# Layer 1's first ten weight quadrants decoded beside layer 0's output products, kept in DRAM, with layer 1's input sums issued twice as fast

## The chip, the cores and the metric

The kernel runs on one NeuronCore of a Trainium2 chip. The metric is the device time in microseconds (us) of one execution. The engines are named as in the profile: PE is TensorE (matmuls; PEld its weight loads), DVE is VectorE, ACT is ScalarE, POOL is GpSimd, and SP is SyncE, which here issues nearly all transfers between DRAM and SBUF, in order, in one queue.

## What is computed

```python
x = attention(q, k, v)            # 4 batches, 12 heads, 448 tokens, head 64, with rms norms and a softmax
x = x.transpose(0, 2, 1, 3).reshape(1792, 768)
x = (x @ w_a) * (x @ w_b) @ w_out                        # layer 0: 768 -> 1536 -> 768
out = (sigmoid(x @ w_gate) * (x @ w_val)) @ w_out2       # layer 1, same sizes
```

The six weight matrices lie in DRAM as 64-bit floats. Everything else is 32-bit.

## The kernel before

**The products.** Each layer has a first part (x times its two left matrices) and a second part (the gated product times the output matrix). Every matrix product is done on quadrants by a scheme of Strassen's kind: seven products of sums of quadrants (passes 1, 2, 5, 3, 6, 7, 4) in place of eight. A 32-bit operand is split into a rounded part and a rest (names ending in h and l, or hi and lo), and each product is three matmuls: high by high, low by high, high by low. So DVE and ACT have to make, for each operand of PE, a cast (ACT: `wh`, `xh`, `gh`) and a subtraction (DVE: `wl`, `xl`, `gl`, in `rest`, line 615).

**First part** (`first_part`, matmuls in line 938). It is a list of 84 events (m, p), m being one of 12 column blocks (even: first matrix, odd: second) and p the pass. An event is 18 matmuls: six steps (two column halves of 512 and 384, by three chunks) of three. The events begin

```python
[(0, 1), (1, 1), (0, 2)] + [(2, 1), (1, 2), (3, 1), (2, 2), (3, 2)] + [(0, 5), (0, 6), (1, 5), (0, 7), (0, 3), ...]
```

and are called e0, e1, ... below: e0 is (0, 1), e4 is (1, 2), e6 is (2, 2), e7 is (3, 2), e8 is (0, 5), e9 is (0, 6), e11 is (0, 7). Passes 1 and 2 share a PSUM bank: after pass 1 of a column block ACT copies the bank away (`u<-mm`, line 990), and pass 2 of the same block adds into the bank, so it cannot begin before that copy. Likewise pass 7 waits for the copy of pass 6 (line 994). e7 thus waits for the copy of e5's bank, e11 for that of e9's. Passes 1 and 2 use quadrants of x as they are; passes 5, 6, 7 and 3 need the sums S1, S2, S3 and S4 of quadrants, which `operands` makes for each layer: per sum three tiles of 128 x 896, each one DVE operation (line 851), one ACT cast (line 842) and one DVE rest. `operands` is advanced once at every fourth step of the first part's events (`ticks % 4`).

**Weights** (`weights`). A quadrant is loaded as pairs of 32-bit words into a `raw` tile (384 KB; two buffers, for layer 1's first ten loads also two of the eight `u` tiles) and decoded to 32-bit floats in a `d` tile by one ACT operation (line 678) and three DVE operations (lines 679, 681, 685). Then `splits` makes `wh` and `wl` of it or of a difference of two quadrants (lines 771 and 775); `wh` and `wl` have four buffers each, so the pair for an event can be written once PE is done with the event four before. `prepare` advances both, at every such step, up to two events ahead of PE. Four quadrants are stored to DRAM (`bd`) after their decoding and loaded again later. Layer 1's decodings begin in the last six groups of layer 0's second part.

**Second part** (`second_part`, line 1221 for layer 0). 42 groups, numbered k: seven passes by six chunks, in layer 0 18 matmuls each. `beside` loads the gated products (`u<-gd`) and the decoded output weights (`d<-wd`), combines them for the pass (lines 1095, 1116) and splits them. At the end of a pass ACT copies the three banks away, and finished quadrants of the result are split into layer 1's operands (`xh`, `xl`). `tick` is called after each three matmuls.

All engines run in order, each through its own list; a row that waits holds everything behind it on that engine.

Of the kernel before, what the change touches and what calls it, by code (L numbers as in the profile page):

```python
# [23 lines left out]
def attention_then_two_gated_mlps(  # L24
# [84 lines left out]
    xd = in_dram("xd", S2, 1, 2, KD)  # L109
    gd = in_dram("gd", S2, 2, 5, HF)  # L110
    wd = in_dram("wd", HB, 2, 6, HF)
    bd = in_dram("bd", HB, 2, 2, 2)


    def attention():
# [516 lines left out]
    Q11, Q12, Q21, Q22 = QUADS = (0, 0), (0, 1), (1, 0), (1, 1)  # L632
    NEEDS = {1: Q11, 5: Q12, 2: Q21, 6: Q22}
    W, done, preps = {}, [-1, -1], [None, None]

    def weights(l):

        plan = []
        events = orders[l]
        k = 0  # L640
        for e, (m, p) in enumerate(events):
            plan.append(("g", m, p))
            while k < 4 * HF and e >= 24 + 2.3 * k:
                plan.append(("o", k % HF, (Q11, Q21, Q12, Q22)[k // HF]))
                k += 1
        assert k == 4 * HF
        wanted = [
            (2, m, p) if x == "o" else (m % 2, m // 2, NEEDS[p]) for x, m, p in plan if x == "o" or p in NEEDS
        ]
        loaded = []  # L650
        total = len(wanted)

        def fill():

            while wanted and len(loaded) < (4 if total - len(wanted) < 10 and len(free_u) >= 3 else 2):
                load()

        def load():
            n, j, q = wanted.pop(0)
            tag = None  # L660
            if [t for t, _ in loaded].count(None) >= 2:
                tag, u = take_u()
                r = u[:, 0:2 * HB].bitcast(U32).rearrange("p (f w) -> p f w", w=2)
            else:
                r = rawp.tile([P, HB, 2], U32, tag="raw", name="raw")
            if n < 2:
                nc.sync.dma_start(out=r.rearrange("p (k f) w -> p k (f w)", f=P), in_=quadrant(l, n, j, q))
            else:
                nc.sync.dma_start(out=r.rearrange("p f w -> p (f w)"), in_=quadrant(l, n, j, q))
            loaded.append((tag, r))  # L670

        def decode(t):
            tag, r = loaded.pop(0)
            t = t.bitcast(U32)
            low, high = r[:, :, 0], r[:, :, 1]


            nc.scalar.activation(out=f32(t), in_=f32(high), func=AF.Copy, scale=2.0 ** -112)  # L678
            nc.vector.tensor_scalar(out=low, in0=low, scalar1=29, scalar2=None, op0=ALU.logical_shift_right)
            yield  # L680
            nc.vector.scalar_tensor_tensor(  # L681
                out=low, in0=high, scalar=0x80000000, in1=low, op0=ALU.bitwise_and, op1=ALU.bitwise_or
            )
            yield
            nc.vector.scalar_tensor_tensor(  # L685
                out=t, in0=t, scalar=3, in1=low, op0=ALU.logical_shift_left, op1=ALU.bitwise_or
            )
            if tag:
                free_u.append(tag)
            fill()  # L690
            yield

        def dec(tag):
            return decp.tile([P, HB], F32, tag=tag, name=tag)

        def less(out, a, b):
            nc.gpsimd.tensor_tensor(out=out, in0=a, in1=b, op=ALU.subtract)

        B, stores = {}, []

        def decodes():
            e = k = -1
            if l == 0:
                fill()
                yield
            else:
                for n in range(12):
                    if n % 3 == 0:
                        load()
                    yield  # L710
            for x, m, p in plan:
                now = stores[:]
                if x == "o":
                    k += 1
                    t = dec("d5" if k % 2 else "d8")
                    yield from decode(t)
                    stores.append((wd[l][QUADS.index(p)][m], t))
                else:
                    e += 1
                    if p in NEEDS:  # L720
                        q = QUADS.index(NEEDS[p])
                        spilled = 2 <= m < EARLY and p < 3
                        tag = f"d{4 * (m % 2) + (q + 1 if spilled else q)}"
                        if q == 1 and m >= EARLY:
                            tag = "d1"
                        if l == 1:
                            while held[0] is not None and tag not in held[0]:
                                yield
                            if held[0] is not None:
                                held[0].remove(tag)  # L730
                        t = dec(tag)
                        B[m, q] = t
                        yield from decode(t)
                        if spilled:
                            stores.append((bd[l][m % 2][q // 2], t))
                for dst, t in now:
                    nc.sync.dma_start(out=dst, in_=t)
                    stores.pop(0)
                decoded[l] = e
                yield  # L740
            for dst, t in stores:
                nc.sync.dma_start(out=dst, in_=t)
            decoded[l] = NE

        again = []

        def reload(m, q):
            B[m, q] = dec(f"d{4 * (m % 2) + q}")
            nc.sync.dma_start(out=B[m, q], in_=bd[l][m % 2][q // 2])

        def splits():
            last = None

            def low():
                n, *of = last
                rest(*of, nc.vector)
                done[l] = n

# [140 lines left out]
    def first_part(l, then):  # L899
# [15 lines left out]
        for e, (m, p) in enumerate(events):  # L915
# [18 lines left out]
            for o, size in HALVES:  # L934
                for c in range(KC):
                    hi, lo = X[n_][c]
                    for z, (w, x) in enumerate(((wh, hi), (wh, lo), (wl, hi))):
                        nc.tensor.matmul(  # L938
                            ps[:, o:o + size], w[:, P * c:P * c + P], x[:, o:o + size],
                            start=(p in (1, 5) and c == 0 and z == 0), stop=(c == KC - 1 and z == 2),  # L940
                            skip_group_check=p not in (1, 5),
                        )
                    prepare(l, min(e + AHEAD, NE - 1), 1)
                    if more is None and ready[0]:
                        more = operands(l)
                    if more is not None:
                        ticks += 1
                        if ticks % 4 == 0:
                            next(more, None)
                    if e >= NE - 4:  # L950
                        then(e - NE)
                    yield
# [213 lines left out]
    def second_part(l, step):  # L1166
# [19 lines left out]
            nc.vector.tensor_tensor(out=sums(x, un), in0=sums("a", un), in1=sums(x, un), op=ALU.add)  # L1186

        after, finals, beats = [], [], []

        def tick(k):  # L1190
            step(k)
            beats.append(k)
            if after and (l == 1 or len(beats) % 3 == 0):
                after.pop(0)()
            if l == 0 and k >= NS - 6:
                prepare(1, max(-1, AHEAD - NS + k), 1)

# [151 lines left out]
```

## Time and profile before

| | |
|---|---|
| median of 3 runs | 1232.35 us (1231.51, 1232.35, 1234.49) |
| profiled execution | 1234.08 us; span from first to last instruction 1232.3 us |
| mean granted clock of PE | 0.985 of full speed |
| attention and the start of layer 0 | up to about 336 us |
| layer 0, first part from there, second part | up to 604.9 us, up to 758.8 us |
| layer 1, first part, second part | up to 1071.3 us, up to 1222.6 us |

The busy time of an engine is a share of the span. PE's busy time counts matmuls from start to modelled end, which overlap: what a matmul costs is read from starts, or from how many start in a stretch.

### The profile page before, as it was taken

The numbers are of one execution on the slowest core, as the hardware profiler recorded it, in microseconds if no ns is written. First come the engines' busy times: TensorE is split into PE (matmuls) and PEld (weight loads), VectorE is DVE, ScalarE is ACT, GpSimd is POOL, SyncE is SP. The second block draws the span as 40 slices with busy tenths as digits, with TensorE's granted clock in tenths as the row PEclk, the third lists the DMA queues.
The fourth block names the chain that finished last, engine by engine and source line by source line (L and its number), as shares of the span: only waits on it lengthen the run. The fifth ranks groups of instructions, "written<-read, shape, count | busy, mean of one in ns | idle before, by whom it ended". The sixth has DMA issues, their size and how long they took to land.

```text
span 1232.3 us, 18208 instructions
## 1 busy us (share of the span) xinstructions
PE 1204.8 (98%) x6440; PEld 1018.6 (83%) x6440; DVE 917.6 (74%) x1625; ACT 655.3 (53%) x1275; POOL 157.4 (13%) x241
## 2 busy tenths in 40 slices
PE   7999999999899999999999999999999999999997
PEld 5666666667688888888888888888888888999997
DVE  6788888864976786876668689966877877666672
ACT  5787778864543434444446565544435444445552
POOL 3666667700000000000000000000000000000000
PEclk7999999999799999999999999999999999999999
DMA  4344454427134665653875754234665654677683
GB/s 132 95 130 134 127 168 130 129 66 261 48 111 130 186 196 142 197 173 126 297 255 165 222 182 141 83 99 131 190 179 165 196 156 156 237 272 239 192 260 94
DMA packets 141899, 203.01 MB, mean 165 GB/s; under 512 B 23112, under 2 KB 116464, under 8 KB 141808
## 3 DMA queue, kind: packets, MB, share of 16 engines
q1 hardware_dynamic: 141200, 201.43, 52.3%
q8 instruction: 50, 0.82, 0.3%
q10 hardware_dynamic: 480, 0.43, 0.1%
q14 instruction: 41, 0.34, 0.1%
q0 software_dynamic: 128, 0.00, 0.0%
HBM read 147.46 MB, written 54.35 MB: 164 GB/s over the span
## 4 chain that ended last, share of the span: by engine, by line
PE 67%; DVE 3%; ACT 2%; DMA 1%; issue 1%; ACTq 0%; SPq 0%; DVEq 0%
PE mm L938 45%; PE mm L1221 13%; PE mm L1231 10%; DVE xl L615 1%; DMA u<-gd 0%; DMA wd<-d 0%; DVE u L851 0%; ACT gh L1135 0%; ACT xh L842 0%; DVE al L851 0%; DVE wl L615 0%; ACTq L1287 0%; ACT mm L1202 0%; ACT ah L1258 0%; ACT u L992 0%
## 5 line engine op out<-in xcount | busy, mean ns | idle before, releaser
L938 PE MATMUL mm<-xh,wh 128*128 128x512 f32 (+1 forms) x1008 | 370.5, 368 | 4.8 <-ACT u L994 2.0
L938 PE MATMUL mm<-xl,wh 128*128 128x512 f32 (+1 forms) x1008 | 371.4, 368 | 3.5 <-DVE xl L615 3.4
L938 PE MATMUL mm<-xh,wl 128*128 128x512 f32 (+1 forms) x1008 | 372.1, 369 | 1.6 <-DVE wl L615 1.6
L938 PEld LDWEIGHTS mm<-xh,wh 128*128 128x128 f32 x1008 | 191.0, 189 | 30.6 <-ACT u L994 2.4
L938 PEld LDWEIGHTS mm<-xl,wh 128*128 128x128 f32 x1008 | 190.9, 189 | 28.3 <-DVE xl L615 5.5
L938 PEld LDWEIGHTS mm<-xh,wl 128*128 128x128 f32 x1008 | 190.9, 189 | 23.9 <-DVE wl L615 2.9
L615 DVE TENSOR_TENSOR wl<-d,wh 128x384 fp32r<-128x384 f32 x252 | 137.5, 552 | 69.3 <-ACT wh L1098 40.3
L783 ACT CAST wh<-d 128x384 fp32r<-128x384 f32 x168 | 83.0, 514 | 107.4 <-DVE d L771 75.1
L678 ACT ACTIVATE d<-raw 128x384 f32<-128x384 f32 x140 | 76.8, 554 | 80.1 <-DMA raw<-in_moe_w_out_dram 43.3
L685 DVE SCALAR_TENSOR_TENSOR d<-d,raw 128x384 uint32<-128x384 uint32 x140 | 78.7, 562 | 52.2 <-ACT d L678 46.3
L361 ACT ACTIVATE P<-s,nm 128x448 f32<-128x448 f32 x168 | 105.2, 635 | 7.4 <-DVE nm L349 7.1
L1098 ACT CAST wh<-d 128x384 fp32r<-128x384 f32 x84 | 43.2, 514 | 119.8 <-issue 36.8
L349 DVE TENSOR_REDUCE nm<-s 128x1 f32<-128x448 f32 x168 | 97.5, 614 | 4.4 <-PE s L343 4.4
L1231 PE MATMUL mm<-wh,gh 128*128 128x384 f32 x294 | 98.8, 336 | 0.3 <-ACT mm L1202 0.2
L1231 PE MATMUL mm<-wl,gh 128*128 128x384 f32 x294 | 98.6, 335 | 0.0
L1231 PE MATMUL mm<-wh,gl 128*128 128x384 f32 x294 | 98.5, 335 | 0.0
L1221 PE MATMUL mm<-gl,wh 128*128 128x512 f32 x252 | 92.6, 368 | 0.0
L1221 PE MATMUL mm<-gh,wl 128*128 128x512 f32 x252 | 92.4, 366 | 0.0
L1221 PE MATMUL mm<-gh,wh 128*128 128x512 f32 x252 | 91.7, 364 | 0.0
L390 ACT COPY pt<-tr 128x512 f32<-128x512 f32 x96 | 55.0, 573 | 49.7 <-PE tr L374 45.5
L681 DVE SCALAR_TENSOR_TENSOR raw<-raw 128x384 uint32<-128x384 uint32 x140 | 78.4, 560 | 4.0
L1008 DVE TENSOR_TENSOR u<-mm,u 128x896 f32<-128x896 f32 x48 | 52.2, 1087 | 30.7 <-PE mm L938 30.6
(155 smaller groups left out, 1947.5 us busy)
## 6 DMA issues: line engine op xcount, KB each, us to landing
gd<-u SPq DMA_DIRECT2D x60, 448.0 KB
u<-gd SPq DMA_DIRECT2D x60, 448.0 KB
d<-wd SPq DMA_DIRECT2D x132, 192.0 KB
raw<-in_moe_w_out_dram SPq DMA_DIRECT2D x48, 384.0 KB
wd<-d SPq DMA_DIRECT2D x72, 192.0 KB
raw<-in_moe_w_a_dram SPq DMA_DIRECT2D x24, 384.0 KB
raw<-in_moe_w_b_dram SPq DMA_DIRECT2D x24, 384.0 KB
raw<-in_moe_w_val_dram SPq DMA_DIRECT2D x23, 384.0 KB
```

What stands on the lines that cost most here:

```text
L349: nc.vector.tensor_reduce(out=d["nm"][:, t:t + 1], in_=d["ps"][t], axis=AX.X, op=ALU.max, negate=True)
L361: nc.scalar.activation(out=e, in_=d["ps"].pop(t), func=AF.Exp, bias=d["nm"][:, t:t + 1], accum_out=d["sum"][:, t:t + 1])
L390: nc.scalar.copy(out=d["pt"][j][:, w], in_=tr)
L615: eng.tensor_tensor(out=lo, in0=t, in1=f32(hi), op=ALU.subtract)
L678: nc.scalar.activation(out=f32(t), in_=f32(high), func=AF.Copy, scale=2.0 ** -112)
L681: nc.vector.scalar_tensor_tensor(out=low, in0=high, scalar=0x80000000, in1=low, op0=ALU.bitwise_and, op1=ALU.bitwise_or)
L685: nc.vector.scalar_tensor_tensor(out=t, in0=t, scalar=3, in1=low, op0=ALU.logical_shift_left, op1=ALU.bitwise_or)
L783: nc.scalar.copy(out=hi, in_=t)
L938: nc.tensor.matmul(ps[:, o:o + size], w[:, P * c:P * c + P], x[:, o:o + size], start=(p in (1, 5) and c == 0 and z == 0), stop=(c == KC - ...
L1008: nc.vector.tensor_tensor(out=u, in0=ps, in1=u, op=ALU.add)
L1221: nc.tensor.matmul(ps[:, o:o + size], w[:, P * un:P * un + P], g[:, o:o + size], start=(p in (1, 5) and f == 0 and z == 0), stop=(f == HF ...
L1231: nc.tensor.matmul(ps[:, o:o + HB], g[:, P * t:P * t + P], w, start=(p in (1, 5) and f == 0 and z == 0), stop=(f == HF - 1 and z == 2), sk ...
```

## The change

Ten quadrants of layer 1's left matrices, those that its first events need (in order: for e0 to e9), are decoded during layer 0's second part instead of at the seam between the layers. A generator `decode_soon` is advanced at every third `tick` of that part (18 matmuls are six ticks, so twice per group) from group 4 on. It takes one of the eight `u` tiles, loads the quadrants through the two `raw` buffers, decodes them into the tile's two halves in turn, and stores each to a DRAM tile of `pd`. At the seam layer 1 loads the decoded quadrants from `pd` (192 KB each) into their `d` tiles; the four that were spilled to `bd` are loaded again from `pd`, without a store of their own. The rule that let layer 1's first ten loads run four ahead goes. And layer 1's `operands` is advanced at every second step of the events instead of every fourth.

```diff
-    bd = in_dram("bd", HB, 2, 2, 2)
+    bd = in_dram("bd", HB, 2, 2)
+    SOON = 10
+    pd = in_dram("pd", HB, SOON)
...
+    soon = [(m % 2, m // 2, NEEDS[p]) for m, p in orders[1] if p in NEEDS][:SOON]
...
+    def decode_soon():
+        raws, late = [], []
+        n_loaded = [0]
+        def load():
+            raws.append(rawp.tile([P, HB, 2], U32, tag="raw", name="raw"))
+            load_raw(raws[-1], 1, *soon[n_loaded[0]])
+            n_loaded[0] += 1
+        def store():
+            n, t = late.pop()
+            nc.sync.dma_start(out=pd[n], in_=t)
+        load()
+        load()
+        while len(free_u) < 2:
+            yield
+        tag, spare = take_u()
+        for n in range(SOON):
+            t = spare[:, HB * (n % 2):HB * (n % 2) + HB]
+            yield from decode_steps(t, raws.pop(0))
+            late.append((n, t))
+            if n_loaded[0] < SOON:
+                load()
+            yield
+            store()
+            yield
+        free_u.append(tag)
...
+        known = {w: n for n, w in enumerate(soon)} if l else {}
         wanted = [
-            (2, m, p) if x == "o" else (m % 2, m // 2, NEEDS[p]) for x, m, p in plan if x == "o" or p in NEEDS
+            (2, m, p) if x == "o" else (m % 2, m // 2, NEEDS[p])
+            for x, m, p in plan
+            if x == "o" or p in NEEDS and (m % 2, m // 2, NEEDS[p]) not in known
         ]
...
-            while wanted and len(loaded) < (4 if total - len(wanted) < 10 and len(free_u) >= 3 else 2):
+            while wanted and len(loaded) < (4 if l == 0 and total - len(wanted) < 10 and len(free_u) >= 3 else 2):
...
-            if l == 0:
-                fill()
-                yield
-            else:
-                for n in range(12):
-                    if n % 3 == 0:
-                        load()
-                    yield
+            fill()
+            yield
...
-                        yield from decode(t)
-                        if spilled:
-                            stores.append((bd[l][m % 2][q // 2], t))
+                        if (m % 2, m // 2, NEEDS[p]) in known:
+                            nc.sync.dma_start(out=t, in_=pd[known[m % 2, m // 2, NEEDS[p]]])
+                            yield
+                        else:
+                            yield from decode(t)
+                        if spilled and l == 0:
+                            stores.append((bd[m % 2][q // 2], t))
...
-            nc.sync.dma_start(out=B[m, q], in_=bd[l][m % 2][q // 2])
+            src = pd[known[m % 2, m // 2, QUADS[q]]] if l else bd[m % 2][q // 2]
+            nc.sync.dma_start(out=B[m, q], in_=src)
...
-                        if ticks % 4 == 0:
+                        if ticks % (2 if l else 4) == 0:
...
+        soon_steps = decode_soon() if l == 0 else None
...
+            if l == 0 and 4 <= k < NS - 6 and len(beats) % 3 == 0:
+                next(soon_steps, None)
```

`load_raw` and `decode_steps` (not shown) are the old loading and decoding code as functions: in a step ACT's operation and DVE's first, in the next DVE's second, in the next DVE's third. PE's and POOL's instructions stand in the same order as before. Line numbers of the changed kernel are its own: its lines 617, 823, 882, 891, 1002, 1030 are 615, 783, 842, 851, 962, 990 of before, and its 649, 650, 652, 656 are 678, 679, 681, 685.

**DVE, start of layer 1's first part.** Before, from the weight rest of e6 (`wl<-d_8624`) over that of e7 (`wl<-d_8656`):

```order
L615 TENSOR_TENSOR wl<-d_8624,wh 128x384
L679 TENSOR_SCALAR raw<-raw 128x384
L681 SCALAR_TENSOR_TENSOR raw<-raw 128x384
L685 SCALAR_TENSOR_TENSOR d_8770<-d_8770,raw 128x384
L615 TENSOR_TENSOR xl<-al,xh 128x896
L851 TENSOR_TENSOR u_8787<-al,ah 128x896
L851 TENSOR_TENSOR al<-ah,al 128x896
L962 TENSOR_TENSOR u_8715<-mm,u_8715 128x896
L771 TENSOR_TENSOR d_8493<-d_8728,d_8493 128x384
L615 TENSOR_TENSOR wl<-d_8656,wh 128x384
L615 TENSOR_TENSOR xl<-al,xh 128x896
L679 TENSOR_SCALAR raw<-raw 128x384
```

Line 962 is the gate of e4 (it reads e4's bank), and line 771 makes e8's difference in `d_8493`. In the changed kernel, the rows around the weight rest of e6 (`d_8666`) up to that of e7 (`d_8699`); e8's difference is made in `d_8509`:

```order
L617 TENSOR_TENSOR xl<-u_8751,xh 128x896
L891 TENSOR_TENSOR u_8806<-al,ah 128x896
L891 TENSOR_TENSOR al<-ah,al 128x896
L617 TENSOR_TENSOR xl<-al,xh 128x896
L617 TENSOR_TENSOR wl<-d_8666,wh 128x384
L617 TENSOR_TENSOR xl<-u_8774,xh 128x896
L617 TENSOR_TENSOR xl<-al,xh 128x896
L617 TENSOR_TENSOR xl<-u_8806,xh 128x896
L1002 TENSOR_TENSOR u_8777<-mm,u_8777 128x896
L811 TENSOR_TENSOR d_8509<-d_8790,d_8509 128x384
L617 TENSOR_TENSOR wl<-d_8699,wh 128x384
L650 TENSOR_SCALAR raw<-raw 128x384
```

The decodings ahead of e7's rest are gone, and the last sums of x (line 891) and all six rests of S4 and S3 now stand ahead of the gate of e4 (line 1002), of the difference for e8 (line 811) and of e7's rest; most of them stood behind these before.

**ACT, the same place.** Before, from the cast for e7 (`d_8656`) to the copy of e5's bank (`u_8840`):

```order
L783 CAST wh<-d_8656 128x384
L678 ACTIVATE d_8770<-raw 128x384
L842 CAST xh<-al 128x896
L783 CAST wh<-d_8493 128x384
L842 CAST xh<-al 128x896
L678 ACTIVATE d_8817<-raw 128x384
L842 CAST xh<-al 128x896
L990 COPY u_8840<-mm 128x896
```

In the changed kernel, from the cast for e7 (`d_8699`) to the copy of e5's bank (`u_8887`):

```order
L823 CAST wh<-d_8699 128x384
L882 CAST xh<-al 128x896
L882 CAST xh<-u_8806 128x896
L823 CAST wh<-d_8509 128x384
L649 ACTIVATE d_8871<-raw 128x384
L1030 COPY u_8887<-mm 128x896
```

In both, the copy of e5's bank stands behind the cast for e8 (of `d_8493`, now `d_8509`), which needs DVE's difference. What moved is that the casts of the last sum of x now stand ahead of that cast.

**DVE, layer 0's second part, end of pass 2.** Before, from the left rest of group 15 to the weight rest of group 15 (the first `wl` is group 14's):

```order
L615 TENSOR_TENSOR gl<-u_7433,gh 128x896
L615 TENSOR_TENSOR xl<-al,xh 128x896 x3
L1095 TENSOR_TENSOR d<-d 128x384
L615 TENSOR_TENSOR wl<-d,wh 128x384
L1116 TENSOR_TENSOR fl<-u_7502,fl 128x896
L615 TENSOR_TENSOR gl<-u_7467,gh 128x896
L1095 TENSOR_TENSOR d<-d 128x384
L615 TENSOR_TENSOR wl<-d,wh 128x384
```

Now, the same stretch:

```order
L617 TENSOR_TENSOR gl<-u_7458,gh 128x896
L617 TENSOR_TENSOR xl<-al,xh 128x896
L656 SCALAR_TENSOR_TENSOR u_7327<-u_7327,raw 128x384
L617 TENSOR_TENSOR xl<-al,xh 128x896 x2
L1135 TENSOR_TENSOR d<-d 128x384
L617 TENSOR_TENSOR wl<-d,wh 128x384
L1156 TENSOR_TENSOR fl<-u_7534,fl 128x896
L617 TENSOR_TENSOR gl<-u_7495,gh 128x896
L650 TENSOR_SCALAR raw<-raw 128x384
L652 SCALAR_TENSOR_TENSOR raw<-raw 128x384
L1135 TENSOR_TENSOR d<-d 128x384
L617 TENSOR_TENSOR wl<-d,wh 128x384
```

One operation of a decoding now stands between the three `xl`, and two more stand ahead of group 15's weight rest.

## Rows read from the trace of the kernel before

**Rows 1.** The page: engines' busy time, and the decoding's ACT operation (busy us, mean ns).

```profile
PE 1204.8 (98%) x6440; PEld 1018.6 (83%) x6440; DVE 917.6 (74%) x1625; ACT 655.3 (53%) x1275; POOL 157.4 (13%) x241
...
L678 ACT ACTIVATE d<-raw 128x384 f32<-128x384 f32 x140 | 76.8, 554 | 80.1 <-DMA raw<-in_moe_w_out_dram 43.3
```

**Rows 2.** Stretches: length; busy (xcount) of PE, PEld, DVE, ACT, POOL; PE clock; DMA share; GB/s.

```profile
803.47:1071.27 267.80, 267.80 (x1315) 239.06 (x1316) 195.49 (x349) 121.18 (x203) 0.00 (x0) 1.00 0.53 164
758.83:803.47 44.64, 41.23 (x200) 35.55 (x199) 42.39 (x60) 27.32 (x40) 0.00 (x0) 1.00 0.26 83
604.80:758.83 154.03, 154.03 (x758) 137.16 (x757) 116.24 (x160) 83.80 (x117) 0.00 (x0) 1.00 0.66 215
```

**Rows 3.** Timeline of PE, all its waits from 758.8 us to 815 us.

```profile
784.90 0.50 PE L938 MATMUL mm<-xh,wh 128*128 128x512 f32 x1 [0.31 <-ACT u L990]
...
793.56 0.50 PE L938 MATMUL mm<-xh,wl 128*128 128x512 f32 x1 [0.60 <-DVE wl L615]
...
797.97 0.50 PE L938 MATMUL mm<-xh,wl 128*128 128x512 f32 x1 [0.48 <-DVE wl L615]
...
803.47 0.50 PE L938 MATMUL mm<-xh,wh 128*128 128x512 f32 x1 [2.03 <-ACT u L994]
```

**Rows 4.** Timeline of DVE in layer 1's first events (start, duration).

```profile
766.03 1.09 DVE L615 TENSOR_TENSOR xl<-al,xh 128x896 fp32r<-128x896 f32 x1
767.15 1.09 DVE L851 TENSOR_TENSOR al<-al 128x896 f32<-128x896 f32 x1
...
775.25 0.35 DVE L679 TENSOR_SCALAR raw<-raw 128x384 uint32<-128x384 uint32 x1
...
779.76 1.09 DVE L962 TENSOR_TENSOR u<-mm,u 128x896 f32<-128x896 f32 x1
780.76 0.55 DVE L771 TENSOR_TENSOR d<-d,d 128x384 f32<-128x384 f32 x1
781.23 0.55 DVE L615 TENSOR_TENSOR wl<-d,wh 128x384 fp32r<-128x384 f32 x1
```

**Rows 5.** Timeline of ACT in layer 1's first events.

```profile
759.02 0.91 ACT L1258 COPY ah<-mm 128x896 f32<-128x896 f32 x1 [0.29 <-PE mm L1221]
...
762.68 0.91 ACT L990 COPY u<-mm 128x896 f32<-128x896 f32 x1 [1.91 <-PE mm L938]
...
763.95 0.50 ACT L783 CAST wh<-d 128x384 fp32r<-128x384 f32 x1
764.35 0.94 ACT L842 CAST xh<-al 128x896 fp32r<-128x896 f32 x1
...
768.53 1.28 ACT L997 ACT_TABLE_LOAD   x1
...
783.97 0.89 ACT L990 COPY u<-mm 128x896 f32<-128x896 f32 x1
```

**Rows 6.** Timeline of DVE in layer 0's second part, end of pass 2.

```profile
648.39 1.09 DVE L615 TENSOR_TENSOR xl<-al,xh 128x896 fp32r<-128x896 f32 x1 [3.83 <-ACT xh L618]
...
653.43 0.55 DVE L615 TENSOR_TENSOR wl<-d,wh 128x384 fp32r<-128x384 f32 x1
...
656.37 0.55 DVE L615 TENSOR_TENSOR wl<-d,wh 128x384 fp32r<-128x384 f32 x1
```

**Rows 7.** Timeline of SP's queue: issues in layer 0's second part.

```profile
608.95 0.50 SPq L1057 DMA_DIRECT2D u<-gd  x1
...
642.69 0.51 SPq L1057 DMA_DIRECT2D u<-gd  x1
```

**Rows 8.** Timeline of ACT: the cast of what SP asked for at 608.95.

```profile
613.73 0.94 ACT L1135 CAST gh<-u 128x896 fp32r<-128x896 f32 x1 [1.17 <-DMA u<-gd]
```

**Rows 9.** Stretches at the start of layer 0, columns as in rows 2.

```profile
335.00:336.00 1.00, 0.21 (x2) 0.07 (x1) 1.00 (x2) 1.00 (x2) 0.00 (x0) 0.59 0.00 0
...
342.00:343.00 1.00, 1.00 (x6) 0.82 (x5) 0.97 (x4) 1.00 (x3) 0.00 (x0) 1.00 0.00 0
```

**Rows 10.** Timeline of PE at the same place.

```profile
335.93 0.80 PE L938 MATMUL mm<-xl,wh 128*128 128x512 f32 x1 [0.79 <-DVE xl L615]
```

More of the change, by code (lines that the diff above doesn't have):

```diff
@@ L634, in attention_then_two_gated_mlps, with load_raw, decode_steps @@
     W, done, preps = {}, [-1, -1], [None, None]
+    soon = [(m % 2, m // 2, NEEDS[p]) for m, p in orders[1] if p in NEEDS][:SOON]
+    def load_raw(r, l, n, j, q):
+        if n < 2:
+            nc.sync.dma_start(out=r.rearrange("p (k f) w -> p k (f w)", f=P), in_=quadrant(l, n, j, q))
+        else:
+            nc.sync.dma_start(out=r.rearrange("p f w -> p (f w)"), in_=quadrant(l, n, j, q))
+    def decode_steps(t, r):
+        t = t.bitcast(U32)
+        low, high = r[:, :, 0], r[:, :, 1]
+        nc.scalar.activation(out=f32(t), in_=f32(high), func=AF.Copy, scale=2.0 ** -112)
+        nc.vector.tensor_scalar(out=low, in0=low, scalar1=29, scalar2=None, op0=ALU.logical_shift_right)
+        yield
+        nc.vector.scalar_tensor_tensor(
+            out=low, in0=high, scalar=0x80000000, in1=low, op0=ALU.bitwise_and, op1=ALU.bitwise_or
+        )
+        yield
+        nc.vector.scalar_tensor_tensor(
+            out=t, in0=t, scalar=3, in1=low, op0=ALU.logical_shift_left, op1=ALU.bitwise_or
+        )
+    def decode_soon():
[23 more added lines that the diff above has]
+        free_u.append(tag)
     def weights(l):
@@ L665, in load @@
                 r = rawp.tile([P, HB, 2], U32, tag="raw", name="raw")
-            if n < 2:
-                nc.sync.dma_start(out=r.rearrange("p (k f) w -> p k (f w)", f=P), in_=quadrant(l, n, j, q))
-            else:
-                nc.sync.dma_start(out=r.rearrange("p f w -> p (f w)"), in_=quadrant(l, n, j, q))
+            load_raw(r, l, n, j, q)
             loaded.append((tag, r))
@@ L673, in decode @@
             tag, r = loaded.pop(0)
[L674 to L679, printed above, removed]
-            yield
-            nc.vector.scalar_tensor_tensor(
-                out=low, in0=high, scalar=0x80000000, in1=low, op0=ALU.bitwise_and, op1=ALU.bitwise_or
-            )
-            yield
-            nc.vector.scalar_tensor_tensor(
-                out=t, in0=t, scalar=3, in1=low, op0=ALU.logical_shift_left, op1=ALU.bitwise_or
-            )
+            yield from decode_steps(t, r)
             if tag:
@@ L702, in decodes @@
             e = k = -1
-            if l == 0:
-                fill()
-                yield
-            else:
-                for n in range(12):
-                    if n % 3 == 0:
-                        load()
-                    yield
+            fill()
+            yield
             for x, m, p in plan:
@@ L732, in decodes @@
                         B[m, q] = t
-                        yield from decode(t)
-                        if spilled:
-                            stores.append((bd[l][m % 2][q // 2], t))
+                        if (m % 2, m // 2, NEEDS[p]) in known:
+                            nc.sync.dma_start(out=t, in_=pd[known[m % 2, m // 2, NEEDS[p]]])
+                            yield
+                        else:
+                            yield from decode(t)
+                        if spilled and l == 0:
+                            stores.append((bd[m % 2][q // 2], t))
                 for dst, t in now:
```

## The prediction

> **What bounds the kernel now.** The page first: PE is busy for 98% of the span [rows 1], so time can only be won where PE waits, or where its clock is down, and lost wherever something new makes it wait. The stretches say where that is. From 803.47 us layer 1's first part runs its last 73 events in 267.80 us, 3.668 us each, at full clock [rows 2]. Layer 0's second part takes 154.03 us for 42 groups, 3.667 us each: the same 18 matmuls at the same pace, so PE never waits there. Between them, from 758.83 to 803.47 us, PE works off 11 events, e0 to e10, in 44.64 us; at 3.668 they need 40.35. So the seam between the layers costs 4.29 us, and that is all that the edits here can win: 0.35% of the kernel. DVE is busy for 42.39 of these 44.64 us [rows 2], ACT for 27.32, the transfers for 26%. PE's own rows show four waits: 0.31 us at e7 for the copy of e5's bank, 0.60 and 0.48 us for the weight rests of e9 and e10, and 2.03 us at e11 for the copy of e9's bank [rows 3]. DVE is what ends last: the two copies are late because ACT stands in front of them at casts whose inputs DVE has not made.
>
> **What is removed at the seam.** Per quadrant, DVE's three operations: the first starts at 775.25 [rows 4], and with its two followers occupies DVE for about 1.3 us; ACT's takes 0.55 us [rows 1]. Ten quadrants are 13 us of DVE and 5.5 us of ACT, of which about half lies before 758 us, where PE does not wait. The rest is what should free PE. The ten loads of 192 KB that take their place lie on transfer engines that are 26% busy [rows 2], and every tile but two is free before e0 begins; the last two (for e8 and e9) wait for the weight rests of e3 and e6 and are wanted, by the times below, 25 and 7 us later. I cost them at nothing; without that cover it would be one transfer, below 5 us by the nearest rows [rows 7, 8].
>
> **What is moved at the seam.** `operands` at twice the pace draws DVE's 24 sums and rests of x together, ahead of weights that PE wants sooner. I follow DVE's new order from the point where it can't start earlier: the third bank of layer 0's result is copied at 759.02 to 759.93 [rows 5], so the third tile of S1 is ready at 761.0. Then the weight rest of e3 (0.47 us; a rest lasts 0.55, but the next starts 0.47 on, as 780.76 and 781.23 show [rows 4]) and the first `xl` end at 762.6, the first tile of S2 at 763.6. The next `xl` needs an ACT cast that stands behind the copy of e0's bank (762.68 [rows 5]) and the cast for e4: copy, cast and cast start at 762.68, 763.5 and 763.9, so the `xl` starts at 764.87. From there DVE has no more reason to wait, and its rows cost 1.00 us per 896 columns (779.76 to 780.76), 1.12 where an in-place sum follows the rest of the same tile (766.03 to 767.15), 0.47 per 384 columns [rows 4]:
> - up to the last `xl` of S2, with e4's rest: 764.87 + 1.12 + 1.00 + 1.12 + 1.00 + 0.47 + 5 x 1.00 = 774.6;
> - two sums, e5's rest, five more of 896: e5's rest ends at 777.15, in time for the third matmul of e5 (777.6); e6's rest starts at 782.1 and ends at 782.6. PE wants it at 758.83 + 6 x 3.668 + 0.47 = 781.3. **PE waits 1.4 us in e6**;
> - three `xl`, the gate of e4: 782.55 + 4 x 1.00 = 786.56, where the difference for e8 begins, ready at 787.1.
> ACT has by then been standing at e8's cast, and behind it are a decoding and the copy of e5's bank: 787.15 + 0.4 (cast, 763.95 to 764.35 [rows 5]) + 0.46 (decoding) + 0.9 (copy) = 788.95. e7 accumulates on that bank. e6 ends at 786.0, so **PE waits 3.0 us for e7**, which begins 788.95 - (758.83 + 7 x 3.668) = 4.45 us late, where the four waits of before add up to 4.29. After it DVE has no sums of x left, e8 to e11 find their weights 3 us and more ahead, and the copy of e9's bank (ready about 801) comes before e11 (803.6). ACT's table load (1.28 us at 768.53 [rows 5]) lies inside its wait for DVE. So the loss is not removed: four waits become two, of the same sum. Net +0.2 us, with 1.5 us either way for the 25 durations and two ACT waits chained above.
>
> **What is added in layer 0's second part.** Ten decodings, one per two groups, from group 4 to about group 24: 1.3 us of DVE in 7.33 us, where DVE is busy 116.24 of 154.03 us [rows 2], so on average it fits (75% becomes 93%). The tight place is the end of pass 2: DVE waits 3.83 us for a cast that waits for PE's last matmuls, then does three `xl`, and only then the weight rest of group 14, which ends at 653.98 [rows 6]; the group begins at 604.80 + 14 x 3.667 = 656.1, a slack of 2.2 us. The decoding's operation between the first two `xl` fits into DVE's wait for the next cast. Two more (0.86 us) come ahead of group 15's rest: before it starts at 656.37 [rows 6], now about 657.2 and done by 657.8, against 659.8: 2.0 us left. Groups 16 to 18 keep 2.4, 2.7 and 3.4 us by the same count. So PE waits for nothing: 0 us. If a raw load comes late, ACT stands in front of it and the slack is spent; each is issued one decoding and a half ahead, some 9 us, and the nearest row to its landing, in the busiest stretch, is 4.8 us from issue (608.95) to the cast that waited for it (613.73) [rows 7, 8]. SP now also stands at the load that needs the buffer freed between the three `xl`, to about 650.7; a transfer issued at 642.69 before [rows 7] goes out near 652, lands by 657 and is wanted by DVE at 661. Below nothing it cannot be, since PE does not wait there now; above, 2 us of lateness more than I count would cost about 3 us.
>
> **The clock.** At the start of layer 0 PE's granted clock fell from 2.4 to 1.2 GHz in the stretch 335 to 336 (0.59) and was back at 342 to 343 (1.00) [rows 9], after a few matmuls between waits, the last of 0.79 us [rows 10]; some 6 us at half clock, in which dense work loses half: at most 3 us. At the seam before, 2.03 us of waiting [rows 3] did not lower it (1.00 in the stretch [rows 2]). The new wait of 3.0 us, with 1.4 us of waiting one event earlier, lies beyond that. The price is between 0 and 3 us; I take 2, since the low level can begin before PE resumes. The Trainium skill (TensorE: Matmul & The Clock Gate, "Why this matters for your kernels") warns of idle gaps between bursts of matmuls, after which the clock goes back to its lower level: it speaks for the fall, and against gathering four waits into two; by it the sum is +2.2 us, by the row of 2.03 us +0.2. No row before shows a wait of this length.
>
> **The rivals.**
> - *The clock holds* (0.27). The wait is as worked out, and PE resumes at 2.4 GHz, as after the 2.03 us [rows 3]: 1232.35 + 0.2 = 1232.5 us.
> - *The seam is relieved* (0.13). The copy of e5's bank comes before e7 wants it (784.5), because DVE's chain runs 4 us shorter than I count: then nearly all of 4.3 us is won, 1228.3 us. For it: some 6 us of decodings leave DVE ahead of e8's difference, which stood at 780.76 before [rows 4]. Against it: 12 sums and rests of 1.00 us that stood behind it come in ahead, and 780.76 - 6 + 12 = 786.8 is the same as the chain's 786.6.
> - *Layer 0's second part loses* (0.15), the other side. One late raw load or a slower DVE at groups 14 to 18 uses up 2.0 us of slack and PE waits on a weight rest there; from 4 us of lateness on it decides, at 2 us in each of two groups, and a clock fall of 2: 1232.35 + 0.2 + 2 + 4 = 1238.6 us.
>
> **How the numbers follow.** The forecast (0.45) is the first sum with a fall of the clock: 0.2 + 0 + 2.0 = +2.2 us. Against the profiled execution's own 1234.08 us that is 1236.3; this execution lay 1.7 us above the median of the runs, so on the median 1232.35 it is **1234.5 us**. A measurement here can tell 0.3%, 3.7 us, from no change. Faster by more than that needs the whole of the relief: 0.09. Slower by more (from 1236.05) is the third rival and the upper end of the forecast, a full 3 us of clock with 1.5 us of error in the chain: 0.19. Within it: 0.72. The range from 1230.0 to 1237.5 leaves out most of the relief and the worst of the third rival. The likeliest case alone spans 1232.5 to 1237.
>
> **What would show it.** Right: two waits of PE at the seam, in e6 for a weight rest and at e7 for the copy of e5's bank (line 1030), together 4 to 5 us; none at e9 to e11; DVE without a pause from 765 to 787; ACT idle before the cast for e8; ten decodings spread over layer 0's second part with no PE wait, and a dip of the clock after e7 begins. Wrong: e7 on time, a wait of PE between 604 and 759 us, or a wait on a transfer from `pd`.

## The result, and the profile after

The changed kernel takes 1240.65 us, median of 6 runs (1236.33 to 1242.66), beside 1232.45 us of the kernel before: a ratio of 1.0057 with a 95% interval of 1.0044 to 1.007. It is 0.57% slower; 1234.5 us was forecast, with 1237.5 as the upper end.

The profiled execution took 1241.96 us, its span is 1240.2 us, 7.9 us more than before. From the page of the changed kernel, as [rows 1]:

```profile
PE 1208.3 (97%) x6440; PEld 1021.6 (82%) x6440; DVE 917.4 (74%) x1625; ACT 654.3 (53%) x1275; POOL 157.1 (13%) x241
```

DVE and ACT have as much to do as before; PE has the same 6440 matmuls. So the loss is waiting and clock. Two stretches of the changed kernel, layer 0's second part and layer 1's first part (length; busy of PE, PEld, DVE, ACT, POOL; clock; transfers; GB/s):

```profile
604.50:764.72 160.22, 157.03 (x757) 139.44 (x757) 122.19 (x173) 85.74 (x121) 0.00 (x0) 0.98 0.70 235
764.72:1079.35 314.63, 309.96 (x1513) 275.71 (x1513) 231.86 (x396) 147.15 (x238) 0.00 (x0) 0.99 0.47 146
```

The first was 154.03 us [rows 2], or 154.14 from first matmul to first matmul, now 160.22: 6.1 us lost where the prediction counted nothing. The second was 312.4 us (44.64 + 267.80 [rows 2]), or 312.3 from first matmul to first matmul, now 314.6: 2.2 to 2.4 us lost, close to the 2.2 forecast. The rest of the program differs by -0.5 us.

All of PE's waits in these two stretches, in its timeline, with the rows on either side of the first:

```profile
670.23 0.33 PE L1264 MATMUL mm<-gh,wl 128*128 128x384 f32 x1
673.75 0.80 PE L1264 MATMUL mm<-gh,wh 128*128 128x512 f32 x1 [3.19 <-ACT al L1289]
674.34 0.63 PE L1264 MATMUL mm<-gl,wh 128*128 128x512 f32 x1
...
679.61 0.34 PE L1264 MATMUL mm<-gh,wh 128*128 128x384 f32 x1
...
788.76 0.50 PE L978 MATMUL mm<-xh,wl 128*128 128x512 f32 x1 [1.62 <-DVE wl L617]
795.29 0.57 PE L978 MATMUL mm<-xh,wh 128*128 128x512 f32 x1 [3.06 <-ACT u L1030]
```

The last two are the seam, and they are the two waits that the prediction derived: e6 for its weight rest (1.4 us forecast, 1.62 found) and e7 for the copy of e5's bank (3.0 forecast, 3.06 found). None is left at e9 to e11. The first is new and was not forecast: group 18, the first of pass 3 in layer 0's second part, waits 3.19 us for ACT's copy at line 1289. After it a matmul of 512 columns takes 0.63 us and more, in place of 0.40, until 679.6. The clock of both places (columns as above):

```profile
660.00:680.00 20.00, 16.81 (x71) 14.58 (x70) 18.30 (x27) 10.69 (x16) 0.00 (x0) 0.83 0.84 286
780.00:800.00 20.00, 15.33 (x67) 12.79 (x66) 17.04 (x23) 11.91 (x17) 0.00 (x0) 0.91 0.17 53
```

Here each of the two waits of some 3 us is followed by a few microseconds at 1.2 in place of 2.4 GHz; a mean of 0.83 or 0.91 is a mixture of the two levels. What a fall costs is read from the work behind it: 24 groups from 673.75 to 764.72 take 90.97 us where 24 x 3.667 = 88.0 are needed, so 3.0 us; 77 events from 795.29 to 1079.35 take 284.06 where 77 x 3.668 = 282.4 are needed, 1.6 us.

**Why group 18 waits.** Pass 3 adds to the banks that pass 5 has filled, so line 1289 must have copied a bank to SBUF before group 18 writes into it. ACT of the kernel before, around that copy, and of the changed one:

```profile
668.38 0.95 ACT L1135 CAST gh<-u 128x896 fp32r<-128x896 f32 x1 [0.72 <-DVE u L1116]
669.23 2.63 ACT L1246 COPY al<-mm 128x896 f32<-128x896 f32 x3
```

```profile
668.61 0.95 ACT L1175 CAST gh<-u 128x896 fp32r<-128x896 f32 x1 [1.96 <-DVE u L1156]
669.46 0.55 ACT L649 ACTIVATE u<-raw 128x384 f32<-128x384 f32 x1
...
671.95 0.94 ACT L1175 CAST gh<-u 128x896 fp32r<-128x896 f32 x1 [1.53 <-DVE u L1156]
672.79 2.51 ACT L1289 COPY al<-mm 128x896 f32<-128x896 f32 x3
```

In both the copies stand behind a cast of a gated tile that a later group wants, and that cast waits for a difference on DVE (line 1116, now 1156). Before, the first copy ended about 0.9 us after 669.23, at 670.1, and group 18 began at 604.80 + 18 x 3.667 = 670.8 [rows 2]: a margin of 0.7 us. In the changed kernel the cast starts 67.45 us into the part (671.95 - 604.50) and not 63.58 (668.38 - 604.80): 3.9 us late, less the margin 3.2, and the wait is 3.19. What made it late stands in DVE's timeline of the changed kernel; all decoding operations between groups 14 and 18 are here:

```profile
655.56 0.36 DVE L650 TENSOR_SCALAR raw<-raw 128x384 uint32<-128x384 uint32 x1
655.95 0.56 DVE L652 SCALAR_TENSOR_TENSOR raw<-raw 128x384 uint32<-128x384 uint32 x1
...
659.36 0.55 DVE L656 SCALAR_TENSOR_TENSOR u<-u,raw 128x384 uint32<-128x384 uint32 x1
...
662.78 0.35 DVE L650 TENSOR_SCALAR raw<-raw 128x384 uint32<-128x384 uint32 x1
663.16 0.56 DVE L652 SCALAR_TENSOR_TENSOR raw<-raw 128x384 uint32<-128x384 uint32 x1
...
666.11 0.55 DVE L656 SCALAR_TENSOR_TENSOR u<-u,raw 128x384 uint32<-128x384 uint32 x1
...
667.42 1.09 DVE L1156 TENSOR_TENSOR u<-u,fl 128x896 f32<-128x896 f32 x1 [0.29 <-DMA u<-gd]
...
669.43 0.36 DVE L650 TENSOR_SCALAR raw<-raw 128x384 uint32<-128x384 uint32 x1
669.83 0.56 DVE L652 SCALAR_TENSOR_TENSOR raw<-raw 128x384 uint32<-128x384 uint32 x1
...
670.78 1.08 DVE L1156 TENSOR_TENSOR u<-u,fl 128x896 f32<-128x896 f32 x1
```

DVE has no pause there but the 0.29 us for a transfer. Each of the eight moves what follows by 0.38 to 0.48 us (start to next start), 3.5 us in all; with the 0.29 that is 3.8 of the 3.9.

DVE had no room there before the change either. Three stretches of the kernel before (columns as above; DVE's is the third busy time):

```profile
655.00:660.00 5.00, 5.00 (x27) 4.42 (x26) 5.00 (x8) 1.98 (x3) 0.00 (x0) 1.00 0.95 289
660.00:665.00 5.00, 5.00 (x26) 4.46 (x25) 5.00 (x7) 2.72 (x5) 0.00 (x0) 1.00 0.98 354
665.00:670.00 5.00, 5.00 (x27) 4.42 (x25) 5.00 (x7) 3.08 (x4) 0.00 (x0) 1.00 0.41 129
```

DVE was busy for all of these 15 us, so whatever was put in there made everything behind it late by its whole length.

### The profile page after: what moved, and what is told of

Same layout as the page of the kernel before. It is cut to its first block, busy times and chain, and to the rows that moved or that the text cites. A ratio compares the mean times of both kernels' runs of the same rounds, so it can differ in the third digit from the quotient of the medians.

```text
span 1240.2 us, 18242 instructions
## 1 busy us (share of the span) xinstructions
PE 1208.3 (97%) x6440; PEld 1021.6 (82%) x6440; DVE 917.4 (74%) x1625; ACT 654.3 (53%) x1275; POOL 157.1 (13%) x241
## 4 chain that ended last, share of the span: by engine, by line
PE 69%; DVE 2%; ACT 1%; issue 1%; ACTq 0%; DVEq 0%
PE mm L978 45%; PE mm L1264 13%; PE mm L1274 12%; DVE xl L617 1%; DVE al L891 0%; DVE u L891 0%; ACTq L1330 0%; ACT mm L1245 0%; ACT ah L1301 0%; DVE wl L617 0%; ACT xh L882 0%; ACT al L1291 0%; DVE u L1156 0%; DVE fl L891 0%; DVE u L1002 0%
## 5 line engine op out<-in xcount | busy, mean ns | idle before, releaser
L649 ACT ACTIVATE d<-raw 128x384 f32<-128x384 f32 x134 | 73.5, 553 | 78.1 <-DMA raw<-in_moe_w_out_dram 42.9
L656 DVE SCALAR_TENSOR_TENSOR d<-d,raw 128x384 uint32<-128x384 uint32 x134 | 74.8, 558 | 50.2 <-ACT d L649 44.4
```

What stands on the lines that cost most here:

```text
L656: nc.vector.scalar_tensor_tensor(out=t, in0=t, scalar=3, in1=low, op0=ALU.logical_shift_left, op1=ALU.bitwise_or)
```

## The experiments

The theory: two separate costs. The pace gathers the seam's waits into longer ones; the decoding's DVE work takes more than the 0.7 us that ACT's copies at the end of pass 5 had to spare. Rivals: transfers and SP's queue, any decoding near a boundary of passes, a shared cause. The kernel before had a median of 1233.5 to 1233.6 us beside the experiments, so ratios are compared and not times. "Second part" is layer 0's, "first part" layer 1's, both from the profiled execution, from first matmul to first matmul.

| kernel | median us, runs | ratio to before, 95% | second part | first part | PE's waits |
|---|---|---|---|---|---|
| before | 1232.45, 6 | 1 | 154.1 | 312.3 | 0.31, 0.60, 0.48, 2.03 |
| changed | 1240.65, 6 | 1.0057 (1.0044 to 1.007) | 160.2 | 314.6 | 3.19; 1.62, 3.06 |
| e1 old pace | 1237.15, 8 | 1.0030 (1.0019 to 1.0042) | 159.1 | 310.3 | 3.15; 2.02 |
| e2 pause | 1235.39, 12 | 1.0016 (1.0006 to 1.0026) | 154.1 | 314.4 | 1.62, 3.07 |
| e3 both | 1232.18, 12 | 0.9991 (0.9981 to 1.0) | 154.1 | 311.9 | 2.04 |
| e4 before, new pace | 1239.38, 5 | 1.0048 (1.0036 to 1.006) | 154.1 | 319.5 | 1.53, 3.08, 4.70 |
| e5 work alone | 1239.92, 4 | 1.0056 (1.0042 to 1.007) | 160.0 | 314.6 | 2.80; 1.6, 3.1 |
| e6 transfers alone | 1234.76, 10 | 1.0015 (1.0004 to 1.0025) | 154.1 | 314.6 | 1.6, 3.1 |
| e7 order on ACT | 1237.07, 7 | 1.0032 (1.0021 to 1.0043) | 155.1 | 314.6 | 0.66; 1.6, 3.0 |
| e10 slower | 1239.12, 5 | 1.0041 (1.0027 to 1.0056) | 156.9 | 313.1 | 2.49; 1.61, 3.08 |
| e8 both and tile | 1230.00, 8 | 0.9974 (0.996 to 0.9988) | 154.4 | 308.7 | 0.4 |
| e9 before, tile | 1231.24, 12 | 0.9982 (0.9972 to 0.9992) | 154.1 | 310.6 | 0.31, 0.60, 0.47, 0.36 |
| e11 as e8 | 1229.35, 9 | 0.9967 (0.9956 to 0.9979) | 154.1 | 308.7 | 0.36 |

**e1, the old pace.**

```diff
-                        if ticks % (2 if l else 4) == 0:
+                        if ticks % 4 == 0:
```

> Only the pace of layer 1's sums goes back to one per four matmul groups of three; the ten quadrants are still decoded early. Theory (two separate costs, the pace at the seam and the decoding in layer 0's second part): the 3.06 us wait of PE at 795 us and the clock fall behind it go, the seam costs 1 to 2 us in place of some 4.7 and 2 of clock, while the 3.19 us wait at the start of pass 3 of layer 0's second part stays as it is; 1240.65 - 5 = 1235.6 us, between 1234 and 1237.5. Rival (the seam is late through the loads that took the place of the decodings, or through the sheer number of sums): the waits at the seam keep their sum of about 4.7 us and the time is 1239 to 1241.

PE's two waits in the timeline, and a stretch around the second (columns as before):

```profile
670.91 0.50 PE L1264 MATMUL mm<-gh,wh 128*128 128x512 f32 x1 [3.15 <-ACT al L1289]
...
803.33 0.50 PE L978 MATMUL mm<-xh,wh 128*128 128x512 f32 x1 [2.02 <-ACT u L1034]
```

```profile
800.00:805.00 5.00, 2.98 (x15) 2.40 (x14) 3.68 (x5) 3.34 (x5) 0.00 (x0) 1.00 0.27 80
```

The seam's two waits are gone, the one in the second part is as it was, and the ratio falls by 0.0027, 3.3 us. That is less than the 5 expected: of the four waits of before three are gone, but the longest, 2.03 us at e11 [rows 3], is there again. The early decoding never touched it.

**e2, a pause of the decoding from group 12 to 19.**

```diff
-            if l == 0 and 4 <= k < NS - 6 and len(beats) % 3 == 0:
+            if l == 0 and 4 <= k < NS - 6 and not 12 <= k < 20 and len(beats) % 3 == 0:
```

> Only the early decoding is paused from group 12 to group 19 of layer 0's second part; pace and everything else as after the change. Theory (DVE's added work in groups 12 to 17 makes ACT late for the copy of pass 5's banks): the 3.19 us wait at the start of pass 3 and the low clock after it go, layer 0's second part takes 154 to 155 us, and the time is 1240.65 - 6 = 1234.6 us, between 1233.5 and 1236; the two waits at the seam stay, 1.6 and 3.1 us. Rival (the lateness comes with any decoding near a pass boundary): a wait of 2 to 3 us comes up at another boundary, groups 24 or 30, and the time is 1238 to 1241.

The stretch of the wait, with the pause:

```profile
660.00:680.00 20.00, 20.00 (x100) 17.81 (x99) 17.38 (x24) 11.57 (x17) 0.00 (x0) 1.00 0.62 202
```

The second part takes 154.1 us again, no other boundary of passes gives a wait though all ten quadrants are decoded, and 0.0041 of the ratio, 5.0 us, is won back. The seam is unchanged. As the theory had it.

**e3, pause and old pace.** Both diffs above.

> Pause of the decoding from group 12 to 19 and the pace of one sum per four together. Theory (the two costs are separate and add up): 1240.65 - 5 - 6 = 1229.6 us, between 1228 and 1231.5, faster than both kernels, which is the early decoding's own gain of about 3 us at the seam. Rival (they share a cause, or the seam is not relieved by ten decodings less): 1232 to 1235.

e1 won 0.0027, e2 0.0041, together 0.0066: the costs add up. But it is only 0.0009 below before, 1.1 us, with an interval that reaches 1.0, and not 3 us: by its time the run falls into the rival's range. Of the 3.4 us of waits at the seam [rows 3] only 1.4 are gone, since the wait at e11 remains. In this profiled execution PE came out of that wait at the low clock:

```profile
799.24 0.80 PE L978 MATMUL mm<-xh,wh 128*128 128x512 f32 x1 [2.04 <-ACT u L1034]
```

```profile
800.00:805.00 5.00, 5.00 (x21) 4.25 (x20) 0.47 (x2) 0.82 (x2) 0.00 (x0) 0.74 0.00 0
```

**e4, the new pace in the kernel before.** There the condition is `ticks % 4` for both layers, and becomes that of the change.

> The kernel before with the doubled pace of layer 1's sums alone. Theory (the pace puts 12 sums and rests of 1.00 us ahead of weights that PE wants sooner): the waits at the seam grow from 4.3 us by as much as the ten decodings still add there, up to 6 us, with a fall of the clock of about 2: 1236 to 1241 us, likeliest 1239. Rival (without the early decoding the weights' steps hold DVE in the old order and the pace changes little): 1231.5 to 1233.5.

PE's waits at the seam:

```profile
778.18 0.50 PE L938 MATMUL mm<-xh,wl 128*128 128x512 f32 x1 [1.53 <-DVE wl L615]
...
785.17 0.50 PE L938 MATMUL mm<-xh,wl 128*128 128x512 f32 x1 [3.08 <-DVE wl L615]
793.35 0.52 PE L938 MATMUL mm<-xh,wh 128*128 128x512 f32 x1 [4.70 <-ACT u L990]
```

9.3 us in place of 3.4 [rows 3], and the first part takes 319.5 us in place of 312.3. The pace by itself costs 0.0048; with the early decoding it costs 0.0025 to 0.0027 (e2 against e3, the changed kernel against e1).

**e5 and e6, the decoding's work and its transfers apart.** e5 keeps two raw tiles and stores one half tile, which layer 1 reads for all ten:

```diff
+            if n_loaded[0] < 2:
                 raws.append(rawp.tile([P, HB, 2], U32, tag="raw", name="raw"))
                 load_raw(raws[-1], 1, *soon[n_loaded[0]])
+            else:
+                raws.append(kept[n_loaded[0] % 2])
...
+        kept = raws[:]
...
-            nc.sync.dma_start(out=pd[n], in_=t)
+            if n == 1:
+                nc.sync.dma_start(out=pd[n], in_=t)
...
-                            nc.sync.dma_start(out=t, in_=pd[known[m % 2, m // 2, NEEDS[p]]])
+                            nc.sync.dma_start(out=t, in_=pd[1])
```

e6 decodes only the first two:

```diff
-            yield from decode_steps(t, raws.pop(0))
+            if n < 2:
+                yield from decode_steps(t, raws.pop(0))
+            else:
+                yield
+                yield
```

> The changed kernel with the decoding's work in layer 0's second part but almost without its transfers: two quadrants are loaded and decoded again and again, one half tile is stored, and layer 1 reads that one for all ten (so the output is not the reference's). Theory (DVE's three operations per decoding, in groups that leave DVE little room, make ACT late for the copy of pass 5's banks): the wait at the start of pass 3 stays, 2.0 to 3.3 us, with the low clock behind it, layer 0's second part takes 158 to 160 us and the time is within 2 us of the changed kernel's, some 0.4 to 0.6% above the kernel before. Rival (the raw loads and the stores on SP's queue, which hold the loads of gated tiles): no wait there, layer 0's second part takes 154 us, time 0.0 to 0.2% above before.

> The counterpart: all ten raw loads and all ten stores at the same places, a tile of u held as long, but only the first two quadrants decoded (the other eight stores hold what these left, so the output is not the reference's). Theory (DVE's work): no PE wait at the start of pass 3, layer 0's second part takes 154 to 155 us, and what is left is the seam's 2 us: 0.1 to 0.25% above before. Rival (transfers and SP's queue, or one tile of u less): the wait stays at 1 to 3.2 us with a low clock behind it, 0.4 to 0.6% above before.

PE of e5 at group 18, and e6's stretch around that place:

```profile
672.10 0.79 PE L1269 MATMUL mm<-gh,wh 128*128 128x512 f32 x1 [2.80 <-ACT al L1294]
```

```profile
660.00:680.00 20.00, 20.00 (x100) 17.82 (x99) 16.55 (x22) 11.62 (x16) 0.00 (x0) 1.00 0.79 258
```

The work alone gives the wait and the changed kernel's time (1.0056 against 1.0057). All ten loads, all ten stores and the tile of `u` held as long, without the work, give no wait, with the transfer engines at 0.79. Transfers, SP's queue and the tile fall as causes; the 0.4 us between 2.80 and 3.19 is about the 0.29 us that DVE waited for a transfer, and 2.80 is the 3.5 us of work less the margin of 0.7.

**e7, all the decoding, another order on ACT.** The step of a gated tile (DVE's difference, ACT's cast of it, and the rest of the tile before) isn't drawn in group 17 but later, so on ACT the copies come ahead of that cast. On DVE the same operations stand in another order:

```diff
-                if (max(d) if d else -1) < min(k + n, NS - 1):
+                if (max(d) if d else -1) < min(k + n, NS - 1) and not (l == 0 and k == 17 and it is left):
```

> The changed kernel with all of the decoding in its place; only the casts of gated tiles are not drawn during group 17, so that on ACT the copies of pass 5's banks stand ahead of the cast that waited for DVE. Theory (PE waits for the copy because it stands behind that cast): the 3.19 us wait at the start of pass 3 goes, and with it the low clock; layer 0's second part takes 154 to 155 us, the time is 0.1 to 0.2% above before, as with the pause. Rival (DVE is simply too late for pass 3, and the copy was only the first to show it): PE waits 1 to 3 us in groups 18 to 21 for a rest of a gated tile, and the time is 0.3 to 0.6% above before.

```profile
669.35 0.50 PE L1264 MATMUL mm<-gh,wh 128*128 128x512 f32 x1 [0.66 <-ACT al L1289]
```

With the same work on DVE, 2.5 of the 3.2 us are gone and the clock stays at 1.00 from 660 to 680 us: it was the place of the copy behind that cast. Groups 18 and after wait for nothing else, so DVE was not too late for pass 3 itself. The ratio, 1.0032, lies above the 1.001 to 1.002 expected, and 2.0 us above e2's; the second part accounts for 1.0 of these (155.1 against 154.1 us), and what the rest is stays open.

**e10, the decoding at every fourth tick.** `len(beats) % 3` in the decoding's condition becomes `% 4`.

> The changed kernel with the decoding's steps at every fourth tick in place of every third, without a pause. Theory (the lateness at the start of pass 3 is the decoding's DVE work since the end of pass 2, 3.5 us of it and 0.3 of transfers, less a margin of 0.7): with three quarters of the work it is 2.6 + 0.3 - 0.7 = 2.2 us, between 1.7 and 2.5, with the low clock behind it; 0.45 to 0.6% above before. Rival (any decoding there upsets the order on ACT, whatever its amount): 3 us and more. If the lateness is in the transfers that gated tiles wait for, it goes below 1.5 us.

PE's waits, and the two stretches around them:

```profile
671.91 0.50 PE L1264 MATMUL mm<-gh,wh 128*128 128x512 f32 x1 [2.49 <-ACT al L1289]
...
790.87 0.50 PE L978 MATMUL mm<-xh,wh 128*128 128x512 f32 x1 [3.08 <-ACT u L1030]
```

```profile
660.00:680.00 20.00, 17.51 (x86) 15.31 (x85) 18.18 (x27) 11.51 (x18) 0.00 (x0) 1.00 0.84 284
780.00:800.00 20.00, 15.31 (x74) 13.06 (x74) 17.71 (x28) 9.79 (x16) 0.00 (x0) 1.00 0.25 86
```

The wait follows the amount of work. DVE's trace has six decoding operations in place of eight ahead of the difference, 2.76 us, and 0.39 us for a transfer; less 0.7 that is 2.45, and 2.49 was found. The low clock that was expected behind it isn't there in the profiled execution, the fastest of the five (1236.33 us).

**e8, e9 and e11, the tile behind e11's wait.** e1 and e3 showed the same 2 us at e11 as [rows 3]. ACT and DVE of the kernel before there:

```profile
800.00 0.94 ACT L842 CAST xh<-u 128x896 fp32r<-128x896 f32 x1
802.51 0.91 ACT L994 COPY u<-mm 128x896 f32<-128x896 f32 x1 [1.57 <-DVE xl L615]
```

```profile
801.33 1.09 DVE L615 TENSOR_TENSOR xl<-u,xh 128x896 fp32r<-128x896 f32 x1
```

The copy of e9's bank waits for a rest of x that has nothing to do with its input: `flush` puts the `u` tile that the rest reads first in the list of free ones, and the copy takes just that tile to write to. The edit puts it last in layer 1, in e8 and e11 on top of e3, in e9 in the kernel before:

```diff
-                    free_u.insert(0, tag)
+                    free_u.insert(len(free_u) if l else 0, tag)
```

> The pause and the pace of one sum per four, as in the run with both; besides, layer 1's tile of u that a rest of x has read is put behind the other free tiles and no more ahead of them. Theory (the 2.03 us wait at e11, which all kernels with the old pace share, is ACT's copy of e9's bank waiting for just the tile that DVE's last rest of x still reads): the copy starts with its predecessor on ACT, 1.5 us and more earlier, the wait shrinks to 0.5 us or less and the clock stays up; 0.3 to 0.4% below before. Rival (the copy is late by its place behind two casts that wait for DVE): the wait stays at about 2 us and the time 0.1% below before.

> The kernel before with the order of free tiles alone: the tile that a rest of x has read goes behind the other free ones in layer 1. Theory (the wait at e11 is a matter of that tile, apart from the early decoding): the 2.03 us wait falls to 0.5 us or less, the three smaller waits at e7, e9 and e10 stay, and the time is 0.10 to 0.15% below before, about half of what the run with pause, old pace and tile gains; the other half is the early decoding's. Rival (the tile helps only where the decoding has left the seam): the wait at e11 stays above 1 us, or comes back at another event, and the time is within 0.05% of before.

> The kernel with pause, old pace and the tile put behind once more, on the chip of the kernel before with the tile alone, so that the two can be told apart. Theory (early decoding and tile add up): 0.2 to 0.35% below before, and 0.1 to 0.2% below the kernel with the tile alone. Rival (one of the two does all): both have the same time within 0.05%.

ACT in e11, and then PE in e11 and in e9:

```profile
796.17 0.94 ACT L882 CAST xh<-u 128x896 fp32r<-128x896 f32 x1
797.01 0.90 ACT L1034 COPY u<-mm 128x896 f32<-128x896 f32 x1
```

```profile
797.97 0.50 PE L978 MATMUL mm<-xh,wh 128*128 128x512 f32 x1 [0.36 <-ACT u L1034]
800.27 0.50 PE L938 MATMUL mm<-xh,wh 128*128 128x512 f32 x1 [0.36 <-ACT u L994]
```

The copy now starts behind its predecessor, and PE's wait falls from 2.0 to 0.36 us, with the decoding early or not. e8 gained 0.26%, a little less than the 0.3 to 0.4 expected. On one chip the tile alone gives 0.9982 and all three edits 0.9967: faster than both kernels by 0.33% and 0.9%. The early decoding's own part is the difference, 0.0015 or 1.9 us; the intervals overlap (0.9972 to 0.9992, 0.9956 to 0.9979), but of the 108 pairs of a run of e11 and one of e9 e11's is the faster in 90, and the waits that it removes, 0.31 + 0.60 + 0.47 = 1.4 us, are in the traces.

## Why the prediction was wrong

- **What bounds the kernel: right in the sizes, with one wrong cause.** The seam's 4.3 us are all that can be won, and e11 leaves 0.6 of them (308.7 us for 84 events that need 84 x 3.668 = 308.1). "The two copies are late because ACT stands in front of them at casts whose inputs DVE has not made" holds for e7. For e11's 2.03 us, half of what there was to win, it does not: there a copy waited for its tile (e9).
- **What is removed at the seam: right.** The loads that took the decodings' place made nobody wait; e1's and e3's seams show the first three waits gone.
- **What is moved at the seam: right in the two waits, to 0.3 us; the comparison with before was not.** 1.4 and 3.0 us were worked out, 1.62 and 3.06 came, at the events and for the releasers named. e1 and e4 show the pace as the cause. But "the four waits of before add up to 4.29" is misread: they add up to 3.42 [rows 3], and 4.29 is by how much e11 is late. So the two new waits are not "of the same sum" but 1.3 us more; by the length of the first part 0.6 to 0.8 us were lost to them (2.2 to 2.4, less the clock's 1.6), where 0.2 was put down.
- **What is added in layer 0's second part: this step failed.** "So PE waits for nothing: 0 us" was concluded from the weight rests of groups 14 to 18, which do come in time. The list of what PE waits for was too short: a group that opens pass 3 also needs its banks copied out, and that copy stood, with 0.7 us to spare, behind a cast that waits for DVE. The average that "fits" (75% becomes 93%) hid that DVE had no pause from 655 to 670 us. A wait of PE between 604 and 759 us was the sign of being wrong that the prediction itself had named. The missing term is 3.5 us of work + 0.3 of transfer - 0.7 = 3.1 us, and 3.19 was found; with the fall of the clock behind it 6.1 us in the profiled execution, and 5.0 by e2's ratio.
- **The rival "Layer 0's second part loses"** (1238.6 us) had the place and the sign, and nearly the price. Its mechanism was another: a weight rest, from 4 us of lateness on. It was a copy, and 0.7 us of lateness was enough.
- **The clock: right at the seam, within its range.** 2 us between 0 and 3 were put down, 1.6 came. That the seam's sum, +2.2 us, is what the first part lost is in part luck: the waits cost 0.4 to 0.6 us more than put down, the clock 0.4 less, and in e10 the clock did not fall at all behind the same wait. The Trainium skill (TensorE: Matmul & The Clock Gate, "Why this matters for your kernels") warned of idle gaps between matmuls; the trace agrees at both places of the changed kernel (0.83 and 0.91). In e10 it does not (3.08 us, 1.00).

## What to carry to other kernels

Before work is put on an engine that "has room", list everything that the waiting engine needs at each boundary of the program, not only its operands: banks to be copied out, buffers to come free. Take for each the time by which it is early now, and for an in-order queue the lateness of everything ahead of it; the smallest such margin (here 0.7 us), and not the engine's average, says how much fits. Where a copy waits for an engine that doesn't make its input, look at which buffer it was given: taking free buffers in the order "last freed, first taken" can cost more (2 us here) than the work that one tries to move.

## What the runs showed of the hardware

Whether the clock falls in a wait is not settled by the wait's length. After 2.0 us at e11 it stayed at 1.00 in the kernel before [rows 2] and in e1, and fell (0.74 in the next 5 us) in e3. After 3.06 us at e7 it fell in the changed kernel (0.91); after 3.08 us at the same event in e10 it stayed at 1.00, as it did after the 3.08 us one event earlier in e4 (1.00 from 777 to 793 us). Where it fell, the work behind took 1.6 us (changed kernel, e7), 1.5 (e3: 269.34 us for 73 events) and 1.9 to 3.0 us longer (group 18 in e1, 89.91 us for 24 groups, and in the changed kernel). That one kernel's runs spread by 6 us (the changed kernel: 1236.33 us at a mean clock of 0.989, 1242.66 at 0.980) fits this, but only profiled executions show the place; for the others it is argued.
